# Six of the eight layernorm transposes of a DiT block: from TensorE through PSUM to a round trip through DRAM with transposing DMA loads

## The chip, the cores and the metric

The kernel runs on one core of a Trainium2 chip. The metric is the device time of one execution in microseconds (us); lower is better.

## The reference

The block takes `x` of 2048 rows by 448. A condition vector gives six modulation vectors (sa, ca, ga, sb, cb, gb). Attention has 16 heads of width 256 over a cached K and V of 2048 positions, without a mask; the MLP is 448 to 1792 to 448 with a gated GELU.

```python
sa, ca, ga, sb, cb, gb = split(silu(c) @ w_mod)
h = layernorm(x) * (1 + ca) + sa
x = x + ga * attention(h @ wq, k_cache, v_cache) @ wo     # 16 heads of 256, 2048 x 2048
h = layernorm(x) * (1 + cb) + sb
x = x + gb * ((gelu(h @ w_gate) * (h @ w_up)) @ w_down)
```

## The kernel before

The rows are handled in four blocks `r` of 512. The attention is a sequence of 64 units, one for each head and block (`u = 4*h + r`), of 16 steps `j`, one for each 128 keys. In each step TensorE computes scores (`st`) two steps ahead and the product with V (`oT`); ScalarE computes the exponentials (`E`); VectorE sums them (`esum`). Side work is hung on a (unit, step) by `fill(u, j, f)`. The instruction order on every engine is fixed by the order of the code, and an engine works through its own stream in order.

```python
for u, (h, r) in enumerate(units):
    ...
    for j in range(NKS):                       # 16 steps
        g = u * NKS + j
        emit_st(g + 2)                         # TensorE, two 128x512 matmuls
        emit_exp(g + 1)                        # ScalarE
        ...                                    # VectorE: esum += E
        for i in range(2):
            nc.tensor.matmul(oT[i][:], lhsT=vs[h][:, j, i * P:(i + 1) * P], rhs=E[:], ...)
        ...
        for f in fills.pop((u, j), ()):        # side work
            f()
        ...                                    # output projection of the last unit: steps 1, 3, 5, 7
```

The matmuls of this kernel contract over the partitions, so the layernorm output h of each block is needed transposed, as `hT` (four chunks of 128 x 512). There are eight such layernorms: a0 to a3 (the blocks of the attention input; a1 to a3 are made during units 0 to 2, just ahead of head 0's q projection of that block) and b0 to b3 (the MLP input; b0 is made during unit 62, b1 to b3 during the MLP of the block before). Before, all eight did it on TensorE: 16 transposes of 128x128 against an identity into PSUM, and four evictions that also modulate, two on VectorE and two on ScalarE. The normalisation of a2 and a3 ran on GpSimd, which needs a shift vector of its own.

```python
def norm(self, t, on_pool=False):
    xn = self.xn[:, t, 0:D]
    if on_pool:
        nc.gpsimd.tensor_scalar(out=xn, in0=..., scalar1=self.rs..., scalar2=self.nm..., ...)   # needs shift()
        return
    nc.vector.tensor_scalar(out=xn, ..., op0=ALU.subtract, op1=ALU.mult)

def transpose(self, pair):                     # pair 0: chunks 0, 1; pair 1: chunks 2, 3
    ...
    tp = self.mi([P, 2, 512], BF16, "tp")      # PSUM
    for i in range(2):
        ch = pair * 2 + i
        for t in range(4):
            nc.tensor.transpose(out=tp[:, i, t * P:(t + 1) * P],
                                in_=self.xn[:, t, ch * P:(ch + 1) * P], identity=id_bf[:])
    for i in range(2):
        ...
        if i == 0:
            nc.vector.tensor_scalar(out=o, in0=a, ...)                       # modulate
        else:
            nc.scalar.activation(out=o, in_=a, func=ACTF.Identity, ...)      # modulate
...
for r in range(NC - 1):
    if r == 0:
        add_ln(0, 0, (0, 1, 2, 3), ("a", 1), x_bf[1], ..., False, (5, 5, 6, 6), (8, 9))
    else:
        add_ln(r, r - 1, (10, 11, 12, 13), ("a", r + 1), x_bf[r + 1], ..., True,
               (0, 0, 0, 0), (7, 8))           # statistics, norms, transposes at these steps
    fill(r, 11, lambda r=r: q_proj(0, r + 1))
```

In the MLP each block runs 14 columns `fc`, in pairs (`gate_up`), then four `down` tiles. The first pair of the next block is issued ahead of this block's `down` (the lead pair). The up projection's PSUM tile rotates over two rings by the column number, and the layernorm steps of the next block are spread over the pairs, four of them to a pair.

```python
def gate_up(r, fc0, hhT):                      # one pair of columns
    for fc in fcs:
        ps[fc, 0] = aps.tile(..., tag="st", bufs=3, name="g_ps")
        if fc % 3 == 2:
            ps[fc, 1] = mi_tile([P, 512], F32, "u_ps")
        else:
            ps[fc, 1] = aps.tile(..., tag="oT", bufs=2, name="u_ps")
    ...                                        # K=64 matmuls of both columns, then K=128 ones
    ...                                        # ScalarE gelu, VectorE hhT = gelu * u_ps

def ln_steps(r):
    ...
    return ([lambda t=t: l.stats(t) for t in range(4)] + [lambda: l.rstd(0, 4)]
            + [lambda: None] + [lambda t=t: l.norm(t) for t in range(4)]
            + [lambda: l.twin(nc.vector)]      # copies the 64-wide last chunk to a full 128
            + [lambda: None] + [lambda p_=p_: l.transpose(p_) for p_ in range(2)])
```

The softmax here doesn't subtract the row's maximum and nothing guards it: scores larger than these inputs give would overflow.

## Time and profile before

| | before |
|---|---|
| time, median of the first 4 runs | 1270.5 us (1270.18 to 1270.78) |
| span of the profiled execution | 1268.5 us |
| TensorE busy | 1249.2 us, 98% |
| busiest other engine | VectorE, 772.8 us, 61% |
| TensorE's recorded waits inside the stream, without the start | about 6 us |

First, from the page of before: the span, the busy times, and the chain of work that ended last.

```profile
span 1268.5 us, 17789 instructions
PE 1249.2 (98%) x6252; PEld 573.6 (45%) x6252; DVE 772.8 (61%) x1611; ACT 712.5 (56%) x1229; POOL 79.1 (6%) x101
...
PE 95%; DVE 3%; ACT 1%; DMA 0%; issue 0%; POOL 0%; SPq 0%; DVEq 0%; POOLq 0%
```

TensorE bounds this kernel. The 98% alone would be weak evidence: the Trainium skill ("Perfetto Trace Analysis", "Identifying the Most-Contended Engine") warns that the busy share of matmuls is a poor measure of how near a kernel is to its limit, because matmuls are pipelined, and in this trace two matmuls of 379 ns each start 0.22 us apart. The chain of waits agrees, though, with 95% of its time on TensorE. So work taken off another engine is worth nothing by itself; what counts is TensorE work and TensorE gaps.

Next, what TensorE waited for in before (columns: engine, program line, what it waited for, us in total, how often, the longest).

```profile
PE oT L474 <- ACT E L434: 2.2, 5, 0.6
PE u_ps L508 <- DVE hhT L521: 2.1, 5, 0.6
...
PE wps L312 <- POOL wo_t L138: 0.5, 1, 0.5
```

These three groups are waits that the change can reach. They are small, so the size of each has to be read from start times in the timeline (columns: start, us, engine, line, what it does, count, and in brackets the idle time before it). Here are eight transposes and the next attention matmuls, from the TensorE timeline of before.

```profile
24.51 0.61 PE L262 MATMUL tp<-id_bf,xn 128*128 128x128 bf16 x8
24.96 0.59 PE L303 MATMUL st<-qT,kT 128*128 128x512 bf16 x2
```

A row's length is not its price. The eight take from 24.51 to 24.96 before the next pair may start, about 0.44 us or 55 ns each. Just after such transposes, in unit 1, there is a gap:

```profile
47.05 0.61 PE L262 MATMUL tp<-id_bf,xn 128*128 128x128 bf16 x8
...
48.35 0.59 PE L303 MATMUL st<-qT,kT 128*128 128x512 bf16 x2
49.59 0.38 PE L474 MATMUL oT<-E,v_h 128*128 128x512 bf16 x1 [0.64 <-ACT E L434]
```

A pair normally starts 0.43 us after the last one; here it took 1.24 us, so the gap costs 0.81. ScalarE was late with the exponential because its two modulating evictions stand before it in the stream, as ScalarE's timeline shows:

```profile
46.59 0.78 ACT L275 ACTIVATE hT<-tp,sa_c,ca1p_c 128x512 bf16<-128x512 bf16 x1 [1.73 <-DVE hT L270]
...
48.27 0.78 ACT L275 ACTIVATE hT<-tp,sa_c,ca1p_c 128x512 bf16<-128x512 bf16 x1 [0.42 <-DVE hT L270]
```

Each took 0.78 us.

The second pattern is in the MLP. First VectorE, then TensorE, in the timeline of before.

```profile
1166.58 0.69 DVE L521 TENSOR_TENSOR hhT<-gl,u_ps 128x512 bf16<-128x512 bf16 x1 [0.61 <-PE u_ps L515]
1167.19 0.62 DVE L224 BATCH_NORM_STATS2 bst<-x_acc 128x6 f32<-128x448 f32 x1
...
1170.12 0.67 DVE L521 TENSOR_TENSOR hhT<-gl,u_ps 128x512 bf16<-128x512 bf16 x1
```
```profile
1169.87 0.38 PE L508 MATMUL g_ps<-hT,wgu 64*128 64x512 bf16 x1
1170.84 0.37 PE L508 MATMUL u_ps<-hT,wgu 64*128 64x512 bf16 x1 [0.60 <-DVE hhT L521]
...
1184.66 0.38 PE L508 MATMUL g_ps<-hT,wgu 64*128 64x512 bf16 x1
1185.35 0.37 PE L508 MATMUL u_ps<-hT,wgu 64*128 64x512 bf16 x1 [0.31 <-DVE hhT L521]
```

Four statistics in a row (1167.19 to 1170.12) stand between two `hhT` products, and the PSUM tile that a product frees comes too late. Elsewhere the second `g_ps` and `u_ps` of K=64 start within 0.01 us of each other. Here `u_ps` started 0.97 us after its `g_ps` (1169.87, 1170.84). The brackets list only 0.60, because they count from the modelled end of the matmul before.

### The profile page before, as it was taken

The page shows a single profiled execution, that of the slowest core. Times are in us where ns is not written, and L with a number is a line of the kernel's source. Part 1 is how long each engine was busy: PE and PEld are TensorE (multiplying, and loading weights), DVE is VectorE, ACT ScalarE, POOL GpSimd, SP SyncE. Part 2 cuts the span into 40 slices and gives each one's busy share as a digit, 9 for nine tenths or more (in the row PEclk, how much of TensorE's full clock was granted, in tenths as well). Part 3 has the DMA queues.
Part 4 walks back from the last instruction along what each step waited for, and adds up shares of the span by engine and source line. Part 5 has one row for each costly group of instructions (what it writes and reads, how often), then busy time and mean ns, then how long its engine had stood idle before and what let it go on. Part 6 is the DMA issues. An engine that isn't in the chain of part 4 may idle for free.

```text
span 1268.5 us, 17789 instructions
## 1 busy us (share of the span) xinstructions
PE 1249.2 (98%) x6252; PEld 573.6 (45%) x6252; DVE 772.8 (61%) x1611; ACT 712.5 (56%) x1229; POOL 79.1 (6%) x101
## 2 busy tenths in 40 slices
PE   6999999999999999999999999999999999999998
PEld 3444444444444444444444444444444444444443
DVE  6766565666656576756566665656665656774443
ACT  4555666656666656556666656665665666642222
POOL 2400000001002020200000000000000000000000
PEclk9999999999999999999999999999999999999999
DMA  9203030713030110403030403011030300000000
GB/s 245 59 9 74 1 81 1 190 44 81 1 81 2 36 46 4 79 1 81 1 82 1 81 1 81 1 36 46 4 79 1 74 1 1 1 1 15 15 15 16
DMA packets 95340, 52.94 MB, mean 42 GB/s; under 512 B 68113, under 2 KB 85714, under 8 KB 95250
## 3 DMA queue, kind: packets, MB, share of 16 engines
q1 hardware_dynamic: 94192, 50.29, 17.1%
q10 hardware_dynamic: 1058, 1.51, 0.4%
q8 instruction: 49, 0.80, 0.3%
q14 instruction: 41, 0.34, 0.1%
HBM read 33.18 MB, written 1.84 MB: 28 GB/s over the span
## 4 chain that ended last, share of the span: by engine, by line
PE 95%; DVE 3%; ACT 1%; DMA 0%; issue 0%; POOL 0%; SPq 0%; DVEq 0%; POOLq 0%
PE oT L474 34%; PE st L303 34%; PE qps L289 9%; PE wps L312 8%; PE dps L526 3%; PE g_ps L515 3%; PE u_ps L515 3%; DVE esum L471 1%; PE g_ps L508 1%; PE tp L262 0%; DMA wm<-in_w_mod_dram 0%; DVE bst L224 0%; DVE hhT L521 0%; PE sps L447 0%; ACT E L434 0%
## 5 line engine op out<-in xcount | busy, mean ns | idle before, releaser
L434 ACT ACTIVATE E<-st 128x512 bf16<-128x512 f32 x1024 | 597.3, 599 | 310.2 <-PE st L303 307.7
L474 PE MATMUL oT<-E,v_h 128*128 128x512 bf16 x2048 | 608.8, 379 | 3.3 <-ACT E L434 2.2
L303 PE MATMUL st<-qT,kT 128*128 128x512 bf16 x2048 | 608.7, 379 | 0.5 <-ACT qT L296 0.5
L471 DVE TENSOR_TENSOR esum<-esum,E 128x512 bf16<-128x512 bf16 x896 | 402.5, 449 | 118.8 <-ACT E L434 74.1
L474 PEld LDWEIGHTS <-v_h 128*128 128x128 bf16 x2048 | 199.7, 98 | 247.3 <-issue 3.9
L303 PEld LDWEIGHTS <-kT 128*128 128x128 bf16 x2048 | 195.3, 98 | 212.9 <-issue 1.5
L317 DVE SCALAR_TENSOR_TENSOR x_acc<-wps,inv,x_acc 128x448 f32<-128x448 f32 x240 | 164.0, 684 | 136.8 <-PE wps L312 136.6
L312 PE MATMUL wps<-wo_t,oTn 128*128 128x448 bf16 x512 | 138.5, 352 | 0.5 <-POOL wo_t L138 0.5
L289 PE MATMUL qps<-hT,wq_t 128*128 128x512 bf16 x512 | 122.2, 381 | 0.2 <-ACT hT L275 0.2
L138 POOL TENSOR_TENSOR wo_t<-wo_t,ga_bf 128x448 bf16<-128x448 bf16 x32 | 35.5, 1131 | 874.8 <-DMA wo_t<-in_A_wo_dram 741.7
L520 ACT ACTIVATE gl<-g_ps 128x512 bf16<-128x512 f32 x56 | 33.4, 597 | 88.4 <-PE g_ps L515 84.4
L296 ACT CAST qT<-qps 128x512 bf16<-128x512 f32 x64 | 37.4, 585 | 76.8 <-PE qps L289 76.8
L289 PEld LDWEIGHTS <-wq_t 128*128 128x128 bf16 x512 | 50.3, 98 | 61.4 <-issue 1.8
L312 PEld LDWEIGHTS <-oTn 128*128 128x128 bf16 x512 | 49.9, 98 | 59.7
L440 DVE CAST oTn<-oT 128x512 bf16<-128x512 f32 x64 | 44.2, 690 | 48.6 <-PE oT L474 48.6
L521 DVE TENSOR_TENSOR hhT<-gl,u_ps 128x512 bf16<-128x512 bf16 x56 | 38.2, 685 | 42.1 <-PE u_ps L515 31.4
L441 ACT CAST oTn<-oT 128x512 bf16<-128x512 f32 x64 | 37.4, 585 | 43.8 <-PE oT L474 43.8
L294 DVE CAST qT<-qps 128x512 bf16<-128x512 f32 x64 | 44.2, 690 | 25.5 <-PE qps L289 25.5
L515 PEld LDWEIGHTS <-wgu 128*128 128x128 bf16 x336 | 30.6, 98 | 48.9 <-issue 15.9
L451 DVE RECIPROCAL inv<-sps 128x4 f32<-128x4 f32 x64 | 11.6, 182 | 65.9 <-PE sps L447 65.9
L515 PE MATMUL g_ps<-hT,wgu 128*128 128x512 bf16 x168 | 45.7, 381 | 0.0
L515 PE MATMUL u_ps<-hT,wgu 128*128 128x512 bf16 x168 | 45.4, 379 | 0.0
(66 smaller groups left out, 317.7 us busy)
## 6 DMA issues: line engine op xcount, KB each, us to landing
wo_t<-in_A_wo_dram SPq DMA_DIRECT2D x16, 224.0 KB, 6.4
wq_t<-in_A_wq_dram SPq DMA_DIRECT2D x16, 192.0 KB, 5.1
out_dram<-ob SPq DMA_DIRECT2D x16, 112.0 KB, 1.7
wd<-in_B_w_down_dram SPq DMA_DIRECT2D x1, 1568.0 KB, 16.5
x_all<-in_A_x_dram SPq DMA_DIRECT2D x3, 448.0 KB, 7.1
wgu<-in_B_w_gate_dram SPq DMA_DIRECT2D x1, 1344.0 KB, 8.8
wgu<-in_B_w_up_dram SPq DMA_DIRECT2D x1, 1344.0 KB, 12.7
wm<-in_w_mod_dram SPq DMA_DIRECT2D x1, 1296.0 KB, 9.1
```

Source lines behind the costliest of these rows:

```text
L289: nc.tensor.matmul(qps[:], lhsT=wq[h][:, ch, dc * P:(dc + 1) * P], rhs=hr[:, ch, :], start=(ch == 0), stop=(ch == DCH - 1),)
L294: nc.vector.tensor_copy(out=qT[:, dc, :], in_=qps[:])
L303: nc.tensor.matmul(st[:], lhsT=kTs[h][:, dc, j * P:(j + 1) * P], rhs=qTs[(h, r)][:, dc, :], start=(dc == 0), stop=(dc == 1),)
L312: nc.tensor.matmul(wps[:], lhsT=oTn[:, dc, t * P:(t + 1) * P], rhs=wos[h][:, dc, :], start=(dc == 0), stop=(dc == 1),)
L317: nc.vector.scalar_tensor_tensor(out=x_acc[r][:, t, :], in0=wps[:], scalar=inv[:, t:t + 1], in1=prev[:, t, :], op0=ALU.mult, op1=ALU.add,)
L434: nc.scalar.activation(out=E[:], in_=sts.pop(g)[:], func=ACTF.Exp, scale=inv_sqrt_dh)
L440: nc.vector.tensor_copy(out=oTn[:, 0, :], in_=oT[0][:])
L471: nc.vector.tensor_tensor(out=esum[:], in0=esum[:], in1=E[:], op=ALU.add)
L474: nc.tensor.matmul(oT[i][:], lhsT=vs[h][:, j, i * P:(i + 1) * P], rhs=E[:], start=(j == 0), stop=(j == NKS - 1),)
L515: nc.tensor.matmul(ps[fc, i][:], lhsT=wgu[:, 3 * i + ch, fc * P:(fc + 1) * P], rhs=hr[:, ch, :], start=False, stop=(ch == 2),)
L521: nc.vector.tensor_tensor(out=hhT[:, fc, :], in0=gl[:], in1=ps[fc, 1][:], op=ALU.mult)
L526: nc.tensor.matmul(dps[:], lhsT=hhT[:, fc, t * P:(t + 1) * P], rhs=wd[:, fc, :], start=(fc == 0), stop=(fc == NHC - 1),)
```

## The change

The intent is to take transposes off TensorE. Six of the eight layernorms (a2, a3, b0 to b3) now store the normalised rows (512 KB) to a DRAM scratch tensor, read them back with four transposing DMA loads, and modulate `hT` in place on VectorE. With that come smaller moves: the normalisation is always on VectorE (GpSimd loses norm and shift); head 0's q projections of blocks 2 and 3 move from step 11 to step 13; MLP statistics of blocks 2 and 3 move into the `down` phase of an earlier block, and those of block 1 into unit 63; in the MLP, norms and the copy to a full 128 (`twin`) come at fixed, mostly earlier columns; and the `u_ps` rotation is driven by a counter that runs on over the blocks.

```diff
+        def turn(self):
+            scr = dram.tile([4 * P, DCH * P], BF16, name="xscr")
+            nc.sync.dma_start(out=scr[:, :].rearrange("(t p) c -> p t c", p=P), in_=self.xn[:])
+            hT[self.key] = hpool.tile([P, DCH, 512], BF16, name="hT")
+            for ch in range(DCH):
+                nc.sync.dma_start_transpose(
+                    out=hT[self.key][:, ch, :], in_=scr[:, ch * P:(ch + 1) * P]
+                )
+
+        def modulate(self, ch):
+            o = hT[self.key][:, ch, :]
+            nc.vector.tensor_scalar(out=o, in0=o, scalar1=self.c1p[:, ch:ch + 1],
+                                    scalar2=self.s[:, ch:ch + 1], op0=ALU.mult, op1=ALU.add)
 ...
-            add_ln(r, r - 1, (10, 11, 12, 13), ("a", r + 1), x_bf[r + 1], ca1p_c, sa_c, True,
-                   (0, 0, 0, 0), (7, 8))
-        fill(r, 11, lambda r=r: q_proj(0, r + 1))
+            add_ln(("a", r + 1), x_bf[r + 1], ca1p_c, sa_c, at(r - 1, 10, 11, 12, 13),   # statistics
+                   at(r, 0, 0, 1, 1), (r, 1), at(r, 12, 12, 13, 13))      # norms, turn, modulations
+            fill(r, 13, lambda r=r: q_proj(0, r + 1))
 ...
-        if h == H - 1 and r == 2:
-            add_ln(u, u, (0, 2, 4, 6), ("b", 0), x_acc[0], cb1p_c, sb_c, False, (8, 9, 10, 11), (13, 14))
+        if h == H - 1 and r in (2, 3):
+            ...                                # b0: turn at unit 62 step 11, modulations in unit 63
 ...
-            if fc % 3 == 2:
+            nu[0] += 1
+            if nu[0] % 3 == 0:
                 ps[fc, 1] = mi_tile([P, 512], F32, "u_ps")
 ...
+    for r in range(2, NC):
+        for t in range(4):
+            mf(r - 2, NHC + t, lambda r=r, t=t: ln2(r).stats(t))          # in down of block r-2
+            mf(r - 1, (2, 3, 3, 4)[t], lambda r=r, t=t: ln2(r).norm(t))   # after these columns
+            mf(r - 1, 9 + t, lambda r=r, t=t: ln2(r).modulate(t))
+        mf(r - 2, NHC + 3, lambda r=r: ln2(r).rstd(0, 4))
+        mf(r - 1, 4, lambda r=r: (ln2(r).twin(nc.vector), ln2(r).turn()))
```

More of the change, by code (lines that the diff above doesn't have):

```diff
@@ L97 @@
     aps = apool("aps", 1, space=bass.MemoryType.PSUM)
+    dram = apool("dram", 2, space=bass.MemoryType.DRAM)
     def mi_tile(shape, dt, name):
@@ L253, in twin @@
             eng.tensor_copy(out=self.xn[:, :, D:DCH * P], in_=self.xn[:, :, 3 * P:D])
+        def turn(self):
[8 more added lines that the diff above has]
+            o = hT[self.key][:, ch, :]
+            nc.vector.tensor_scalar(
+                out=o, in0=o, scalar1=self.c1p[:, ch:ch + 1], scalar2=self.s[:, ch:ch + 1],
+                op0=ALU.mult, op1=ALU.add,
+            )
         def transpose(self, pair):
@@ L354, with add_ln @@
     fill(4, 9, lambda: mod_cols_out(mod_cols(3), sb_c, cb1p_c))
-    def add_ln(u, us, st, key, src, c1p, s, on_pool, jn, jt):
+    def add_ln(key, src, c1p, s, js, jn, jt, jm=None):
         box = {}
@@ L362, in stats, with at @@
             box["l"].stats(t)
-        def rstd():
-            box["l"].rstd(0, 4)
-            if on_pool:
-                box["l"].shift()
         for t in range(4):
-            fill(us, st[t], lambda t=t: stats(t))
-        fill(us, st[3], rstd)
+            fill(*js[t], lambda t=t: stats(t))
+        fill(*js[3], lambda: box["l"].rstd(0, 4))
         for t in range(4):
-            fill(u, jn[t], lambda t=t: box["l"].norm(t, on_pool))
-        fill(u, jn[3], lambda: box["l"].twin(nc.gpsimd if on_pool else nc.vector))
-        for p_ in range(2):
-            fill(u, jt[p_], lambda p_=p_: box["l"].transpose(p_))
+            fill(*jn[t], lambda t=t: box["l"].norm(t))
+        fill(*jn[3], lambda: box["l"].twin(nc.vector))
+        if jm is None:
+            for p_ in range(2):
+                fill(*jt[p_], lambda p_=p_: box["l"].transpose(p_))
+        else:
+            fill(*jt, lambda: box["l"].turn())
+            for ch in range(DCH):
+                fill(*jm[ch], lambda ch=ch: box["l"].modulate(ch))
+    def at(u, *js):
+        return [(u, j) for j in js]
     for r in range(NC - 1):
         if r == 0:
-            add_ln(0, 0, (0, 1, 2, 3), ("a", 1), x_bf[1], ca1p_c, sa_c, False, (5, 5, 6, 6), (8, 9))
-        else:
-            add_ln(r, r - 1, (10, 11, 12, 13), ("a", r + 1), x_bf[r + 1], ca1p_c, sa_c, True,
-                   (0, 0, 0, 0), (7, 8))
-        fill(r, 11, lambda r=r: q_proj(0, r + 1))
+            add_ln(("a", 1), x_bf[1], ca1p_c, sa_c, at(0, 0, 1, 2, 3), at(0, 5, 5, 6, 6), at(0, 8, 9))
+            fill(0, 11, lambda: q_proj(0, 1))
+        else:
+            add_ln(("a", r + 1), x_bf[r + 1], ca1p_c, sa_c, at(r - 1, 10, 11, 12, 13),
+                   at(r, 0, 0, 1, 1), (r, 1), at(r, 12, 12, 13, 13))
+            fill(r, 13, lambda r=r: q_proj(0, r + 1))
     for u, (h, r) in enumerate(units):
@@ L396 @@
             fill(u, 15, lambda h=h, r=r: q_proj(h + 1, r))
-        if h == H - 1 and r == 2:
-            add_ln(u, u, (0, 2, 4, 6), ("b", 0), x_acc[0], cb1p_c, sb_c, False, (8, 9, 10, 11), (13, 14))
+        if h == H - 1 and r in (2, 3):
+            jm = at(u + 1, 4, 6, 8, 10) if r == 2 else [("mlp", ch) for ch in range(DCH)]
+            jn = at(u, 8, 9, 10, 11) if r == 2 else [("n", t) for t in range(4)]
+            add_ln(("b", r - 2), x_acc[r - 2], cb1p_c, sb_c, at(u, 0, 2, 4, 6), jn,
+                   (u, 11) if r == 2 else ("turn", 0), jm)
     mlpw = {}
@@ L493 @@
     wgu, wd = mlpw["gu"], mlpw["d"]
+    nu = [0]
     def gate_up(r, fc0, hhT):
@@ L521, in gate_up @@
             nc.vector.tensor_tensor(out=hhT[:, fc, :], in0=gl[:], in1=ps[fc, 1][:], op=ALU.mult)
+            for f in mfill.pop((r, fc), ()):
+                f()
     def down(r, t, hhT):
@@ L531, in down @@
         nc.vector.tensor_tensor(out=ob[:], in0=dps[:], in1=x_acc[r][:, t, :], op=ALU.add)
+        for f in mfill.pop((r, NHC + t), ()):
+            f()
         row = r * 512 + t * P
         nc.sync.dma_start(out=out2d[row:row + P, :], in_=ob[:])
-    def ln_steps(r):
-        l = LN(("b", r), x_acc[r], cb1p_c, sb_c, mi_tile)
-        return (
-            [lambda t=t: l.stats(t) for t in range(4)] + [lambda: l.rstd(0, 4)]
-            + [lambda: None] + [lambda t=t: l.norm(t) for t in range(4)]
-            + [lambda: l.twin(nc.vector)]
-            + [lambda: None] + [lambda p_=p_: l.transpose(p_) for p_ in range(2)]
-        )
+    mfill = {}
@@ new lines, in mf @@
+    def mf(r, k, f):
+        mfill.setdefault((r, k), []).append(f)
+    ph, pr, po, psums = pend
+    box = {}
+    mf(0, 1, lambda: box.update(inv=psums()))
+    for t in range(4):
+        for f in fills.pop(("n", t)):
+            mf(0, t // 2, f)
+    mf(0, 1, fills.pop(("turn", 0))[0])
+    for t in range(4):
+        mf(0, 1 + 1 + t, lambda t=t: wo_tile(ph, pr, t, po, box["inv"]))
+        mf(0, 9 + t, fills.pop(("mlp", t))[0])
+    for r in range(2, NC):
+        for t in range(4):
+            mf(r - 2, NHC + t, lambda r=r, t=t: ln2(r).stats(t))
[3 more added lines that the diff above has]
+        mf(r - 1, 4, lambda r=r: (ln2(r).twin(nc.vector), ln2(r).turn()))
@@ L544, with ln2, lead @@
+    lns = {}
+    def ln2(r):
+        if r not in lns:
+            lns[r] = LN(("b", r), x_acc[r], cb1p_c, sb_c, mi_tile)
+        return lns[r]
     hhs = {}
     LEAD = 2
-    for r in range(NC):
-        if r not in hhs:
-            hhs[r] = res.tile([P, NHC, 512], BF16, name="hhT", tag="xh", bufs=2)
-        todo = ln_steps(r + 1) if r + 1 < NC else []
-        if r == 0:
-            ph, pr, po, psums = pend
-            box = {}
-            todo = (
-                [lambda: None, lambda: box.update(inv=psums())]
-                + [lambda t=t: wo_tile(ph, pr, t, po, box["inv"]) for t in range(4)] + todo
-            )
-        for fc in range(0 if r == 0 else LEAD, NHC, 2):
+    def lead(r):
+        hhs[r] = res.tile([P, NHC, 512], BF16, name="hhT", tag="xh", bufs=2)
+        for fc in range(0, LEAD, 2):
+            gate_up(r, fc, hhs[r])
@@ L558 @@
+    lead(0)
+    for r in range(NC):
+        for fc in range(LEAD, NHC, 2):
             gate_up(r, fc, hhs[r])
-            for _ in range(4):
-                if todo:
-                    todo.pop(0)()
         if r + 1 < NC:
-            hhs[r + 1] = res.tile([P, NHC, 512], BF16, name="hhT", tag="xh", bufs=2)
-            for fc in range(0, LEAD, 2):
-                gate_up(r + 1, fc, hhs[r + 1])
+            lead(r + 1)
         for t in range(4):
```

## The prediction

> **What bounds it now.** TensorE: 98% busy on the page, 95% of the chain of waits that ended last, clock 1.0. In the timeline matmuls start back to back (a 128x512 pair every 0.43 us), so only TensorE work removed, or its gaps, count. Its recorded waits sum to 16 us, half at the start.
>
> **Removed.** (a) 96 of 128 TensorE transposes (six of eight layernorms). Each is listed at 219 ns, but they overlap: eight between attention matmuls push the next one back 0.44 us, 55 ns each. The Trainium skill ("TensorE: Matmul & The Clock Gate", Part 4) gives about 275 ns for one in a kernel; here duration is not cost. 12 x 0.44 = 5.3 us.
> (b) Gaps after them: the scalar Identity evictions (777 ns) delay exp; TensorE loses 0.81 us in each of units 1 and 2, about 0.8 in unit 62, and 0.5 in the first MLP layernorm, waiting for the twin copy. 2.9 us.
> (c) Four layernorm statistics in a row on VectorE hold up hhT in MLP blocks 1 and 2: gate/up pairs of 4.20 us against 3.23. Moved to the down phase: 1.9 us.
> (d) The u_ps rotation restarts at each block, and the lead pair waits for hhT: 3.82 us to the down matmuls against 3.24 in the last block. The running counter removes 3 x 0.58 = 1.7 us.
> (e) GpSimd loses shift and norms, so wo is scaled sooner: 0.5 us of a TensorE wait.
> Sum 12.3 us.
>
> **Added.** Six 512 KB DRAM stores, 24 transposing loads, 24 in-place modulations on VectorE (estimate 0.36 us, from 0.35 for the 128x448 bf16 norm). Estimated round trip: 3.5 us for the store (112 KB output stores take 1.7), four issues at 0.65 us (2.15 for a four times larger K transpose), 2.8 us to land: chunk 0 after 7 us, the last after 9. The code leaves 11 us in attention, 9 for the first MLP block, 8 to 14 later. The Trainium skill ("DMA: Bandwidth & Descriptors", "Two DMAs through the same engine are not ordered") makes a load of stored data wait for the store's completion, so both are in series.
>
> **New waits.** In units 1 and 2 modulations and the next q projection share step 13, the next unit's first scores follow at step 14. In unit 1 VectorE also has four statistics (0.75 us each) in steps 10 to 13 and lags: stepping through, chunk 2 comes 1.2 us late, then 0.5 us for the scalar copy of qT before the scores (a wait of 0.5 at the start shows it). 1.9 us in unit 1, 0.8 in unit 2. In the MLP the lead pair uses chunk 3 first, just modulated: 0.1 us x 3. Sum 3.0 us.
>
> **Prediction.** 1270.5 - 12.3 + 3.0 = 1261 us; range 1257.5 to 1265.5. Faster by over 2%: 1%; within 2%: 98%; slower: 1%.
>
> **What would show it.** 32 tp transposes left; no 0.6 us oT waits on ACT in units 1 and 2; MLP pairs even at 3.23 us, no u_ps wait on hhT; new TensorE waits of qps on VectorE's hT and of st on ACT's qT, 2 to 3 us together; VectorE waits on the hT DMA near zero.
>
> **What would make it wrong.** A round trip of 12 us or more: VectorE then sits before a modulation and TensorE stops at q_proj or the lead pair, 1 to 4 us each, six times. Or no lag in unit 1: 1259.

## The result, and the profile after

| | before | after |
|---|---|---|
| median time | 1270.31 us (1269.66 to 1274.11, 13 runs) | 1258.55 us (1257.86 to 1259.4, 8 runs) |
| span of the profiled execution | 1268.5 us | 1256.1 us |
| TensorE busy | 1249.2 us | 1241.5 us |
| transposes on TensorE | 128 | 32 |

The ratio is 0.9906, with a 95% interval of 0.9896 to 0.9915: 11.8 us less. A ratio is the mean time of one kernel's fast runs over that of the other's of the same rounds, so it is not quite the ratio of the medians quoted beside it.

The same parts of the page of after:

```profile
span 1256.1 us, 17629 instructions
PE 1241.5 (99%) x6156; PEld 568.1 (45%) x6156; DVE 776.6 (62%) x1633; ACT 705.4 (56%) x1217; POOL 71.2 (6%) x87
...
PE 96%; DVE 2%; ACT 0%; DMA 0%; issue 0%; POOL 0%; SPq 0%; DVEq 0%; POOLq 0%
```

What TensorE waited for in after:

```profile
PE st L321 <- ACT qT L314: 1.2, 3, 0.5
...
PE qps L307 <- DVE hT L268: 0.7, 1, 0.7
PE oT L500 <- ACT E L460: 0.4, 1, 0.4
```

Of the three groups shown for before, the waits on `hhT` and on GpSimd's `wo_t` are gone, and the wait on the exponential fell from 2.2 to 0.4. In their place are the wait of q projections on the modulated `hT`, and scores waiting longer for ScalarE's `qT` (0.5 before). TensorE's busy time fell by 7.7 us, so the span's 12.4 us came partly from work and partly from gaps. The cleanest account is by stretches of the TensorE timeline, from one marker matmul to the next (a unit's stretch ends with its row-sum matmuls, which run just after its last step; an MLP block's ends with its first `down` matmul):

| stretch, us | before | after | difference |
|---|---|---|---|
| unit 0 | 20.25 | 20.25 | 0.00 |
| unit 1 | 21.27 | 20.47 | -0.80 |
| unit 2 | 20.61 | 19.51 | -1.10 |
| units 3 to 61 | 1011.80 | 1011.03 | -0.77 |
| unit 62 | 17.38 | 15.74 | -1.64 |
| unit 62's end to the MLP | 13.80 | 13.79 | -0.01 |
| MLP block 0 to its `down` | 30.21 | 27.99 | -2.22 |
| MLP block 1 | 35.77 | 33.22 | -2.55 |
| MLP block 2 | 35.78 | 33.23 | -2.55 |
| MLP block 3 | 29.99 | 29.99 | 0.00 |

Units 1, 2, 62 and MLP blocks 0 to 2 give 10.9 us, and those stretches repeated within 0.02 us in every later kernel that left their code alone. Units 3 to 61, where nothing was changed, did not: they took 1010.8 to 1011.9 us in the various runs, and 1011.74 in a second profile of after. That 0.77 is stray. Of the rest of the difference between 12.4 and 10.9, about 0.35 is the start (up to the first scores, which varies by as much from run to run), and 0.35 is the end: from block 3's first `down` matmul to the end of the span before, e1 and e2 took 14.41 to 14.44 us, and the eleven other profiles 14.02 to 14.11. So the end is no stray difference. The matmuls and the issues of the output stores there are timed alike in before and after; what comes after them is shorter, and why is not shown.

The round trip, in after: first SyncE's queue in unit 1, then the DMA issues over the whole program (size of one, and us from its issue to landing).

```profile
39.54 0.39 SPq L259 DMA_DIRECT2D xscr<-xn  x1
42.48 5.97 SPq L262 DMA_TRANSPOSE hT<-xscr  x4
```
```profile
xscr<-xn SPq DMA_DIRECT2D x6, 512.0 KB, 2.9
...
hT<-xscr SPq DMA_TRANSPOSE x24, 2.7
```

The first transposing load was issued 2.94 us after the store, when the store had landed. This trace agrees with the Trainium skill ("DMA: Bandwidth & Descriptors", "Two DMAs through the same engine are not ordered"), which has a dependent load wait on the first transfer's semaphore: the two legs are in series. The four issues took 5.97 us of SyncE's queue here; over the program one took 1.25 us at the median. From the issue of the store to the landing of the last chunk, the trace has 10.4 us in unit 1 (39.54 to 49.98) and 9.5 to 9.9 in the five other places. VectorE has no listed wait for these loads in after, so the round trip is hidden in all six places.

Where it did cost something is the end of unit 1. TensorE, then VectorE, in the timeline of after:

```profile
49.92 0.59 PE L307 MATMUL qps<-hT,wq_t 128*128 128x512 bf16 x2
51.22 1.56 PE L307 MATMUL qps<-hT,wq_t 128*128 128x512 bf16 x6 [0.71 <-DVE hT L268]
52.70 0.38 PE L321 MATMUL st<-qT,kT 128*128 128x512 bf16 x1
53.46 0.38 PE L321 MATMUL st<-qT,kT 128*128 128x512 bf16 x1 [0.38 <-ACT qT L314]
```
```profile
49.05 0.73 DVE L268 TENSOR_SCALAR hT<-hT,ca1p_c,sa_c 128x512 bf16<-128x512 bf16 x2
49.70 0.62 DVE L225 BATCH_NORM_STATS2 bst<-x_all 128x6 f32<-128x448 bf16 x1
...
50.45 0.39 DVE L497 TENSOR_TENSOR esum<-esum,E 128x512 bf16<-128x512 bf16 x1
50.76 0.73 DVE L268 TENSOR_SCALAR hT<-hT,ca1p_c,sa_c 128x512 bf16<-128x512 bf16 x2
```

The q projection takes 49.92 to 52.70, 2.78 us, where eight of these matmuls without a wait take 1.73 (8 x 0.216). The second pair of modulations was late because VectorE also had a3's statistics in its stream. The next scores then wait for the scalar copy of `qT`: their second matmul starts 0.76 us after the first, against 0.22, which costs 0.54. The two together cost 1.6 us in unit 1 and 0.6 in unit 2.

### The profile page after: what moved, and what is told of

Its sections match the earlier page's. It is cut to its first block, busy times and chain, and to the rows that moved or that the text cites. A ratio compares the mean times of both kernels' runs of the same rounds, so it can differ in the third digit from the quotient of the medians.

```text
span 1256.1 us, 17629 instructions
## 1 busy us (share of the span) xinstructions
PE 1241.5 (99%) x6156; PEld 568.1 (45%) x6156; DVE 776.6 (62%) x1633; ACT 705.4 (56%) x1217; POOL 71.2 (6%) x87
## 4 chain that ended last, share of the span: by engine, by line
PE 96%; DVE 2%; ACT 0%; DMA 0%; issue 0%; POOL 0%; SPq 0%; DVEq 0%; POOLq 0%
PE oT L500 34%; PE st L321 34%; PE qps L307 9%; PE wps L330 8%; PE dps L557 3%; PE g_ps L544 3%; PE u_ps L544 3%; PE g_ps L537 1%; DVE esum L497 1%; DMA wm<-in_w_mod_dram 0%; PE sps L473 0%; DVE oTn L466 0%; DVE bst L225 0%; ACT hT L293 0%; DVE xn L248 0%
```

## The experiments

The experiments ask three things: does each gain come from the part named for it; is VectorE's lag, rather than the DMA round trip, the cause of the new waits (the rival was that the round trip itself is at its limit); and what does the moved GpSimd work do. Each run has a profile and is timed against the kernel before in the same rounds, on one of three chips; before's median in them was 1269.63 to 1270.48 us. All twelve computed the right result. The edits are cut to the parts of lines that differ.

| run | median us | ratio to before (95%) | unit 1 | unit 2 | unit 62 | MLP 0 | MLP 1 | MLP 2 |
|---|---|---|---|---|---|---|---|---|
| before | 1270.31 | | 21.27 | 20.61 | 17.38 | 30.21 | 35.77 | 35.78 |
| after | 1258.55 | 0.9906 (0.9896 to 0.9915) | 20.47 | 19.51 | 15.74 | 27.99 | 33.22 | 33.23 |
| e1_counter | 1266.70 | 0.9976 (0.9963 to 0.9990) | 21.28 | 20.61 | 17.38 | 29.52 | 35.09 | 34.26 |
| e2_stats_in_down | 1267.64 | 0.9984 (0.9972 to 0.9997) | 21.28 | 20.61 | 17.38 | 30.21 | 34.80 | 34.81 |
| e3_mlp_on_pe | 1261.34 | 0.9930 (0.9918 to 0.9943) | 20.48 | 19.50 | 15.74 | 28.88 | 34.12 | 34.12 |
| e4_att_on_pe | 1262.08 | 0.9937 (0.9924 to 0.9949) | 20.61 | 20.62 | 17.39 | 27.98 | 33.23 | 33.23 |
| e5_late | 1267.54 | 0.9982 (0.9969 to 0.9994) | 26.03 | 23.83 | 15.74 | as after | | |
| e6_stats_early | 1259.27 | 0.9915 (0.9901 to 0.9928) | 21.10 | 19.50 | 15.74 | as after | | |
| e7_all_early | 1258.23 | 0.9909 (0.9896 to 0.9923) | 19.82 | 18.92 | 15.74 | as after | | |
| e8_shift | 1259.53 | 0.9915 (0.9900 to 0.9930) | 21.34 | 19.50 | 15.74 | as after | | |
| e9_stats_only | 1257.03 | 0.9898 (0.9883 to 0.9913) | 19.50 | 19.49 | 15.74 | as after | | |
| e10_spaced | 1257.72 | 0.9901 (0.9886 to 0.9916) | 20.62 | 18.92 | 15.74 | as after | | |
| e11_after_again | 1258.73 | 0.9908 (0.9892 to 0.9925) | 20.48 | 19.50 | 15.74 | as after | | |
| e12_both | 1257.28 | 0.9898 (0.9881 to 0.9914) | 19.06 | 19.07 | 15.74 | as after | | |

Whole times of runs that are 1 us apart overlap in their intervals, so the verdicts below on effects of that size rest on the stretches, which repeat to 0.02 us, and on the timeline lines.

### The running counter alone, on before

```diff
+    nu = [0]
-            if fc % 3 == 2:
+            nu[0] += 1
+            if nu[0] % 3 == 0:
```

> The kernel before, with the running counter for the u_ps buffers and nothing else of the change. Theory (the gain is a sum of separate TensorE items): the three lead pairs fall from 3.82 us to about 3.13 us, the u_ps waits on hhT halve in number (the two in the pairs behind four statistics stay), and the time falls by 3 x 0.69 = 2.1 us, ratio 0.9984. Rival (the transposing DMA brings everything, the counter only fits the new order): the lead pairs stay at 3.8 us or the stall moves to another pair, ratio 1.000.

Measured: MLP block 0 lost 0.69 us, block 1 lost 0.68, block 2 lost 1.52. The 0.69 is the delay that before's timeline shows in the lead pair (1184.66 to 1185.35), and not the predicted 0.58. Block 2 gained more because with the shifted rotation its statistics hold the late `u_ps` up by only 0.15 us (1206.48 to 1206.63 in this run's timeline); those of block 1 still cost 0.97 (1168.16 to 1169.13). The waits of TensorE say the same: of before's five waits on `hhT`, 2.1 us, one is left.

```profile
PE u_ps L511 <- DVE hhT L524: 0.6, 1, 0.6
```

### The statistics in the down phase alone, on before

```diff
+        if r + 2 < NC:                        # in down(r, t, ...)
+            if t == 0:
+                lnd[r + 2] = LN(("b", r + 2), x_acc[r + 2], cb1p_c, sb_c, mi_tile)
+            lnd[r + 2].stats(t)
+            if t == 3:
+                lnd[r + 2].rstd(0, 4)
 ...
+        head = [lambda: None] * 5             # in ln_steps: placeholders, so that the other steps stay
+        if r not in lnd:
+            head = [lambda t=t: l.stats(t) for t in range(4)] + [lambda: l.rstd(0, 4)]
```

> The kernel before, with the statistics and rstd of MLP row blocks 2 and 3 moved into the down phase of the block before the previous one, and nothing else (transposes stay on TensorE, old buffer rotation). Theory: the two pairs of 4.20 us fall to 3.23 us, minus 1.9 us, ratio 0.9985; lead pairs stay at 3.82. Rival (the jam is VectorE's total load in the block, not the four statistics in a row): the two pairs stay above 3.8 us, ratio 1.000.

Measured: block 1 from 35.77 to 34.80 and block 2 from 35.78 to 34.81, 0.97 us each, which is the delay that the timeline of before shows (1169.87 to 1170.84). The three lead waits of 0.3 us stay:

```profile
PE u_ps L508 <- DVE hhT L521: 0.9, 3, 0.3
```

So before's five waits were two jams from the statistics and three lead pairs. Note that e1 and e2 together gain less than their sum in block 2, since each of them removes that jam.

### After, with b1 to b3 transposed on TensorE again

```diff
-        mf(r - 1, 4, lambda r=r: (ln2(r).twin(nc.vector), ln2(r).turn()))
+        mf(r - 1, 4, lambda r=r: ln2(r).twin(nc.vector))
-            mf(r - 1, 9 + t, lambda r=r, t=t: ln2(r).modulate(t))
+            if t in (0, 2):
+                mf(r - 1, 9 + t, lambda r=r, t=t: ln2(r).transpose(t // 2))
 (the same for b1)
```

> The changed kernel, with the three layernorms of MLP row blocks 1 to 3 transposed on TensorE again (after gate/up columns 9 and 11), keeping counter and moved statistics. Theory: each costs 16 x 55 ns = 0.9 us of TensorE, 2.7 us together, up to 3.3 if the scalar evictions delay the gate activation: slower than the changed kernel by 2.7 to 3.3 us, ratio to before about 0.993. Rival (the transposes hide behind the matmuls, all of the MLP gain is counter and statistics): the same as the changed kernel, ratio 0.9906, MLP blocks of 33.2 us.

Measured: blocks 0, 1 and 2 are longer by 0.89, 0.90 and 0.89 us: 16 transposes cost TensorE 0.89 us, 56 ns each, and with the other repairs in place nothing else. The median is 2.8 us above that of after. The transposes themselves were worth what their start times said. The run shows one thing more. Block 0 took 29.52 us in e1 and takes 28.88 here, with its transposes on TensorE and the counter running in both. So 0.64 us of block 0's gain does not come from taking transposes off TensorE, but from how the side work of that block was moved (statistics, norms and twin copies above all): before's gap of 0.54 us inside block 0's transposes (1141.33 to 1141.87, waiting for the twin copy) is not in this trace.

### After, with a2, a3 and b0 transposed on TensorE again

```diff
-                   at(r, 0, 0, 1, 1), (r, 1), at(r, 12, 12, 13, 13))
-            fill(r, 13, lambda r=r: q_proj(0, r + 1))
+                   at(r, 0, 0, 1, 1), at(r, 7, 8))
+            fill(r, 11, lambda r=r: q_proj(0, r + 1))
 (and b0: transposes at unit 62, steps 13 and 14)
```

> The changed kernel, with the three layernorms made during attention (two of the first head, the first of the MLP) transposed on TensorE again at the steps of the kernel before, q projection back at step 11, norms still on VectorE. Theory: unit 1 changes by little (0.88 us transposes and 0.81 us of exp delay come back, 1.6 us of new waits go), unit 2 longer by 1.1 us, unit 62 by 1.65 us: slower than the changed kernel by about 2.8 us, ratio to before about 0.993. Rival (the attention part gains nothing net, because the new q and st waits eat it): the same as the changed kernel within 0.5 us.

Measured: unit 62 is longer by 1.65 us and unit 2 by 1.11, but unit 1 by only 0.14. In unit 1 the transposes and their gap (0.88 + 0.81) are nearly paid for by the two new waits that the round trip version has there (1.6). So in unit 1 moving the transposes bought almost nothing; that unit's gain of 0.80 against before comes mainly from the GpSimd work that left (see e8).

### The round trip four steps later

```diff
-                   at(r, 0, 0, 1, 1), (r, 1), at(r, 12, 12, 13, 13))
+                   at(r, 4, 4, 5, 5), (r, 5), at(r, 12, 12, 13, 13))
```

> The changed kernel, with the norms and the turn of the two first-head layernorms four steps later (steps 4, 4, 5, 5 instead of 0, 0, 1, 1), about 4.2 us later; modulations and q projections stay. Theory (the round trip is 10.4 us long and ends only about 1 us before the third and fourth chunk are used): VectorE now waits on the DMA of hT before the modulations, TensorE waits about 3 us more at the q projection of unit 1 and about 2.2 us more in unit 2; slower than the changed kernel by 4 to 6.5 us, ratio to before about 0.995. Rival (the DMA has ample slack, VectorE alone sets these waits): within 1 us of the changed kernel, no VectorE wait on the hT DMA.

Measured: units 1 and 2 are longer by 5.56 and 4.32 us, more than the 3 and 2.2 expected. VectorE now waits for the loads, and TensorE for VectorE:

```profile
DVE hT L268 <- DMA hT<-xscr: 7.1, 7, 2.0
```
```profile
PE qps L307 <- DVE hT L268: 6.4, 7, 1.5
```

The direction separates the theories: in after the round trip is not the limit, since no wait on these loads is listed there, but by the landing times little slack is left. The last chunk lands 1.1 us before its modulation starts in unit 1 (49.98, 51.08) and 0.6 in unit 2 (69.22, 69.85).

The size was mis-set, and part of the excess is the clock. Of the traces with a clock record (all but e4's), this is the only one in which the granted clock fell in the middle (line PEclk of this run's page, in tenths for 40 slices):

```profile
PEclk9899999999999999999999999999999999999999
```

Its record has half clock from 53.36 to 60.19 and from 80.67 to 84.08, in and after the two stretches in which TensorE waits; all five executions show a mean clock of 0.996 or 0.997. At half clock five q matmuls took 2.09 us (55.98 to 58.07) instead of 1.08. Estimated from start times in the same way, the slow clock costs about 1.7 us in unit 1 and 1.3 in unit 2. That the waits brought the clock down fits the times, but no run tests it. For the rest, the store was issued 4.1 and 4.7 us later in its unit than in after, and in unit 1 took 4.85 us from issue to the first load instead of 2.9. Why that store was slow is open.

### The statistics of a3 taken out of unit 1's last steps

```diff
-            at(r - 1, 10, 11, 12, 13)
+            at(r - 1, *((10, 11, 12, 13) if r == 1 else (2, 4, 6, 8)))
```

> The changed kernel, with the four statistics of the unit-1 layernorm (for row block 3) at steps 2, 4, 6, 8 of unit 1 instead of 10 to 13. Theory (VectorE's lag from these statistics delays the modulations): the q wait on VectorE's hT of 0.71 us in unit 1 falls to 0.1 or less, unit 1 shorter by 0.9 to 1.0 us (20.47 to about 19.5, as unit 2), st waits on qT unchanged at 0.4 us; ratio 0.990. Rival (the third chunk lands late, the statistics only fill the wait): the wait stays, and VectorE shows a wait on the hT DMA instead.

Measured: unit 1 did not shrink but grew by 0.63 us. Taken at its word this run refutes the lag theory. Its timeline shows what happened, VectorE first, then GpSimd:

```profile
49.38 2.16 DVE L268 TENSOR_SCALAR hT<-hT,ca1p_c,sa_c 128x512 bf16<-128x512 bf16 x2
```
```profile
49.26 2.12 POOL L139 TENSOR_TENSOR wo_t<-wo_t,ga_bf 128x448 bf16<-128x448 bf16 x2
```

Earlier statistics let GpSimd finish the reciprocal root earlier, and so start scaling the next `wo` at 49.26, just when VectorE modulates. The pair of modulations took 2.16 us instead of 0.73. The Trainium skill ("SBUF — State Buffer", "SBUF: two separate sides") says that GpSimd and certain VectorE instructions share a port pair under an exclusive lock, with the loser blocked for the whole instruction; these records fit that: each modulation took 1.1 us, against 0.36 in a pair without GpSimd, and ended 0.15 us after a scaling did. So the experiment had exchanged one delay for another, and had to be repeated without the collision (e9).

### Everything about a2 and a3 earlier

```diff
-                   at(r, 0, 0, 1, 1), (r, 1), at(r, 12, 12, 13, 13))
-            fill(r, 13, lambda r=r: q_proj(0, r + 1))
+                   at(r - 1, 14, 14, 15, 15), (r - 1, 15), at(r, 9, 9, 10, 10))
+            fill(r, 11, lambda r=r: q_proj(0, r + 1))
 (statistics at steps 8 to 11 of unit 0 and at 2, 4, 6, 8 of unit 1)
```

> The changed kernel, with both first-head layernorms pulled forward: statistics at steps 8 to 11 of unit 0 and 2, 4, 6, 8 of unit 1; norms and turn at steps 14 and 15 of the unit before; modulations at steps 9 and 10; the q projection at step 11, three steps before the next unit's scores. Theory (both new waits are distances, not work): no q wait on hT and no st wait on qT in units 1 and 2, minus 1.05 + 0.54 us in unit 1 and 0.62 us in unit 2, so 2.2 us under the changed kernel, about 1256.3 us, ratio 0.9889. Rival (the VectorE work has to be paid somewhere in units 0 to 2): less than half of it appears, and unit 0 gets longer.

Measured: unit 1 is 19.82 and unit 2 18.92, shorter by 0.65 and 0.59, but unit 0 is 2.09 us longer. There VectorE reached the first statistic of a2 before its block of x had been loaded, and stopped 1.55 us for that load. TensorE then waited 2.14 us for an exponential. In ScalarE's stream that exponential (30.02) stood behind an eviction of a1's transposes (29.34), which had waited 1.90 us for VectorE's half of it (28.76), and this stood behind the load in VectorE's stream. In unit 1 a wait of 0.4 us for `hT` was left. What was won in units 1 and 2 was lost in unit 0 (median 1258.23 against 1258.55, no difference).

### GpSimd's shift put back

```diff
+        if key == ("a", 2):
+            fill(*js[3], lambda: box["l"].shift())
```

> The changed kernel, with the two unused GpSimd shift operations of the first unit-1 layernorm put back before the scaling of wo (their result is not used, the output is the same). Theory (the wo wait of before came from these operations standing in front of the scaling): the wo scaling starts 0.5 us later and a TensorE wait of wps on it of 0.3 to 0.5 us comes back in unit 1. Rival (the wait hung on when ga or wo arrived, or on GpSimd sharing time with VectorE): no such wait.

The two small GpSimd operations make something nobody reads. Measured: unit 1 is longer by 0.87 us, 21.34. GpSimd, then TensorE:

```profile
37.09 0.33 POOL L238 TENSOR_SCALAR nm<-nm 128x4 f32<-128x4 f32 x1
37.39 2.31 POOL L139 TENSOR_TENSOR wo_t<-wo_t,ga_bf 128x448 bf16<-128x448 bf16 x2
```
```profile
39.74 0.35 PE L330 MATMUL wps<-wo_t,oTn 128*128 128x448 bf16 x1 [0.70 <-POOL wo_t L139]
```

In after the same scaling starts at 36.05 and this wait does not exist. So the shift in front of the scaling is enough to bring the wait back. In before itself the wait was worth 0.66 us (the first output matmuls start 0.85 us apart, against 0.19 without it), and it lay on the critical path although GpSimd is busy 6% of the time.

### The statistics of a3 earlier, without the collision

```diff
-            at(r - 1, 10, 11, 12, 13)
+            at(r - 1, *((10, 11, 12, 13) if r == 1 else (2, 4, 6, 13)))
```

The last statistic stays at step 13, so GpSimd's work stays where it is in after.

> The changed kernel, with three of the four unit-1 statistics at steps 2, 4 and 6, the last one left at step 13 (after the q projection), so that GpSimd cannot finish the layernorm's rstd early and its scaling of wo stays where it was. The run with all four early was confounded: the scaling moved to 49.3 us and two modulations took 2.16 us against 0.73. Theory (VectorE's lag makes the q wait): modulations at 0.73 us a pair, q wait of 0.71 us falls to 0.1 or less, unit 1 from 20.47 to about 19.5 us; ratio 0.990. Rival (the third chunk lands too late whatever VectorE does): the q wait stays above 0.5 us, with VectorE waiting on the hT DMA.

Measured: unit 1 is 19.50, shorter by 0.97 us. The modulations take 0.73 us a pair again, and the q projection runs through:

```profile
49.01 0.73 DVE L268 TENSOR_SCALAR hT<-hT,ca1p_c,sa_c 128x512 bf16<-128x512 bf16 x2
```
```profile
50.48 1.89 PE L307 MATMUL qps<-hT,wq_t 128*128 128x512 bf16 x8
```

This is what e6 was meant to show: the wait of unit 1's q projection in after is VectorE's lag from a3's statistics. The round trip was not touched, and the wait went. But it is now close to its limit: the last two chunks landed at 49.44 and 50.00, and their modulations started at 49.99 and 50.31.

### a3 spaced out, and unit 1's scores reordered

```diff
-                   at(r, 0, 0, 1, 1), (r, 1), at(r, 12, 12, 13, 13))
+                   *((at(1, 0, 0, 1, 1), (1, 1), at(1, 12, 12, 13, 13)) if r == 1 else
+                     (at(1, 14, 14, 15, 15), (1, 15), at(2, 9, 9, 10, 10))))
+            late = (u, j) == (1, 14)          # scores after the product with V at this step
+            if not late:
+                emit_st(g + 2)
 ...
+            if late:
+                emit_st(g + 2)
```

with a3's statistics at steps 2 to 5 and its q projection at step 11.

> The changed kernel with the new waits spaced out: the unit-1 statistics at steps 2 to 5, so that rstd and the scaling of wo on GpSimd are over before the modulations of step 12; the layernorm for row block 3 normed and turned at steps 14 and 15 of unit 1, modulated at steps 9 and 10 of unit 2, its q projection at step 11; and at step 14 of unit 1 the first scores of the next unit after the oT matmuls instead of before them. Theory: unit 0 unchanged at 20.25, unit 1 about 19.1 us (q wait gone, 0.43 of the 0.54 us st gap filled), unit 2 18.92 us as in the run that pulled everything forward; together 1.9 us under the changed kernel, about 1256.6 us. Rival (GpSimd and VectorE still meet and give it back): unit 1 stays at 20 us or more.

Measured: unit 2 fell to 18.92, and in unit 1 the wait for `qT` is gone, filled by the product with V. But unit 1 as a whole is 20.62. GpSimd's scaling moved to 46.51, and five sums that it overlapped took 3.52 us, so the modulations began at 50.50 instead of 49.05 and the q projection waited again (1.0 us listed in all). It is the collision of e6 in another place.

### After once more, in the same rounds

> The changed kernel once more, on the same chip as the two others, to compare with them in the same rounds. Both theories: ratio to before 0.9906, units 1 and 2 at 20.5 and 19.5 us, unless GpSimd and DMA times shift.

Measured: 1258.73 us (1258.21 to 1259.42), with the stretches of after to 0.02 us except units 3 to 61, which took 1011.74 instead of 1011.03 (the first scores, too, started 0.8 us later). This is the measure of what a stray difference is.

### Both repairs

The edit is that of e9, with the reordering of e10 at step 14 of units 1 and 2.

> The changed kernel with the three unit-1 statistics at steps 2, 4 and 6 (GpSimd undisturbed, as in the run that settled the VectorE lag), and at step 14 of units 1 and 2 the next unit's first scores after the oT matmuls. Theory: unit 1 from 20.47 to 19.1 us (0.97 of the q wait and 0.43 of the st gap), unit 2 from 19.5 to 19.1 us, nothing else moves; 1.8 us under the changed kernel, about 1256.7 us, ratio 0.989 or less, no st wait on qT in units 1 and 2. Rival (moving the scores back delays exp, and the loss reappears at the start of the next unit): units 1 and 2 stay at 19.5 us.

Measured: units 1 and 2 are 19.06 and 19.07, shorter than in after by 1.41 and 0.44 us, and both new waits are gone from them, but for 0.2 us between the two first scores (0.40 us apart instead of 0.22). The median is 1257.28, no better than e9's 1257.03, because units 3 to 61 took 0.9 us more than in e9, which is within their stray. The two are the fastest versions run, about 1.4 us under after; the intervals overlap with that of after, so the whole times alone do not prove it.

## Why the prediction was right

The predicted time was 1261 us with a range of 1257.5 to 1265.5, and 1258.55 was measured. The bound, the main mechanisms and the sign of every term but one small one held: the predicted 3 x 0.1 us of waits in the MLP did not come. The gain was put too low by 2.5 us; the terms account for 1.5 of it:

| term | predicted us | measured us | shown by |
|---|---|---|---|
| (a) 96 transposes less | 5.3 | 5.3 | e3, 0.89 for each MLP layernorm |
| (b) gaps after them | 2.9 | about 3.0 | unit 62 (1.64 less 0.88; e4), units 1 and 2 in the timeline, MLP block 0's rest (e3) |
| (c) statistics moved | 1.9 | 1.9 | e2, 0.97 twice |
| (d) running counter | 1.7 | 2.1 | e1, 0.69 three times |
| (e) GpSimd relieved | 0.5 | 0.66 | timeline of before; e8 shows the cause |
| new waits | -3.0 | -2.2 | timeline of after, e9 |
| sum | 9.3 | 10.8 | |

The measured terms sum to 10.8, and the six changed stretches to 10.9, so the account closes there. For each: unit 62 is 0.88 + 0.77. MLP block 0 is 0.89 from transposes, 0.69 from the counter, and a remaining 0.64, for which 0.5 was predicted as the wait for the twin copy. e3 shows that this part belongs to the moved statistics, norms and twin copies and not to the transposes; no run moved any of these alone. Blocks 1 and 2 are 0.89 + 0.69 + 0.97 = 2.55 each, which is exactly what was measured.

- Point (a) held because the price was read from start times, 0.44 us for eight, and not from the 219 ns rows. At 219 ns it would have been 21 us.
- Point (b) named ScalarE's own evictions as what delays the exponential. They do, but ScalarE also waits for VectorE's eviction before each of them (1.73 and 0.42 us in unit 1), which the prediction left out.
- Point (d) was mis-sized. The prediction compared a lead pair of 3.82 us with 3.24 in the last block. The last block's pair takes 1250.89 to 1254.03, that is 3.14, in the same trace. The right 0.69 could also be read as the late start of `u_ps`.
- The step "chunk 2 comes 1.2 us late" was near: the q projection of unit 1 lost 1.05. The step "the lead pair uses chunk 3 first, just modulated: 0.1 us x 3" failed: no such wait is in after, and blocks 1 and 2 close without it. New waits in unit 2 were 0.6 and not 0.8, and those of unit 1 were 1.6 and not 1.9.
- The round trip was estimated at 9 us to the last chunk from a store of 3.5, issues of 0.65 and 2.8 to land. It took 9.5 to 10.4 from a store of 2.9, issues of 1.25 and 2.7. That it came so near is partly luck: the store was put too long and the issues too short. The issue time shrank less than the size, which the estimate from a four times larger load (2.15 us) had not allowed for. In units 1 and 2 about 1 us was left, so a slightly larger error would have mattered; e5 shows the price of being late.
- About 0.9 us of the 11.8 lies in no changed stretch. About 0.35 of it is the shorter end of the program, which repeats in every version built on after. The rest is of the size by which the stretches without a change vary from run to run. No run here assigns either to a part of the change, so their cause stays open.

## What to carry to other kernels

On a bound TensorE, price work by how far it moves the next start, and gaps by start-to-start times, not by the listed durations or waits; summed so, the terms closed to 0.1 us here. About 40% of the gain, before new waits (5.3 of 13 us), came from small companions of the change (the rotation counter, moved statistics, norms and twin copies, two tiny operations off GpSimd), so test these alone before crediting the headline. And when work is moved in time, look at which other engine it releases: two of these experiments failed because an earlier statistic let GpSimd run into VectorE. A single run that misses its expectation may have changed a second thing; e6 would have been read as a refutation without its timeline.

## What the Trainium skill lacked or had wrong

- "TensorE: Matmul & The Clock Gate", Part 4 gives about 275 ns for a transpose in a kernel. The trace lists 219 ns, but back to back between matmuls one costs TensorE 55 ns (0.44 us for eight; 0.89 for 16 in e3). A start-to-start cost of this kind, which decides what moving transposes away is worth, is on the page for matmuls but not for transposes.
- "DMA: Bandwidth & Descriptors", "DMA Transpose (X-bar)" has no time for one transposing load, on the issuing queue or to landing; elsewhere the page has a bandwidth, and a cycle count for small tiles. Here one transposing load of a 128x512 chunk took 1.25 us of SyncE's queue and 2.7 us to land (medians), and a whole store and reload of 512 KB 9.5 to 10.4 us.
- "SBUF — State Buffer", "SBUF: two separate sides" describes the lock, but the page has times only for the reverse case, a GpSimd DMA held up by VectorE, and for VectorE held up by GpSimd a bare factor. Here a modulation on VectorE went from 0.36 to 1.1 us, and the mean sum in e10's five from 0.45 to 0.7, beside a GpSimd scaling of 2.1 to 2.2 us.
